# Induced attention, then a gated channel mix: one step for each token-stage operation, stage B inside one PSUM bank, gate products in the sum's bank, second products four steps behind

## The chip, the cores and the metric

The kernel runs on one core of a Trainium2 chip. Its time is the device time of one execution in microseconds (us); lower is better. The engines are TensorE (PE in the profile, its weight loads PEld), VectorE (DVE), ScalarE (ACT), GpSimd (POOL) and SyncE (SP, which here issues nearly all DMAs).

## The reference, cut to what matters

`x` is [4, 12608, 128] in float32, `inducing` is [32, 128], the hidden layer has 1024 columns.

```python
def mab(q, kv):
    s = scale * (q @ kv.transpose(0, 2, 1))
    s = s - s.max(-1, keepdims=True)
    a = np.exp(s)
    a /= a.sum(-1, keepdims=True) + 1e-09
    return a @ kv
h = mab(I, x)              # 32 inducing points attend to all tokens of a batch
x = mab(x, h)              # every token attends to the 32 rows of h
...
x_prev = x shifted by one token, zero at the start
xk = mu_k * x + (1.0 - mu_k) * x_prev
xr = mu_r * x + (1.0 - mu_r) * x_prev
k = np.maximum(xk @ w_k, 0.0)
v = k * k @ w_v
r = 1.0 / (1.0 + np.exp(-(xr @ w_r)))
return r * v
```

## The kernel before

Each of the four batches is cut into 24 groups of 512 tokens and one of 320. A group takes four **steps** of the main loop, one for each pair of 128-column chunks of the hidden layer, so a batch has 100 steps and the program 400. The second attention is never multiplied out: the mixed weights are multiplied by h beforehand (`W[0]`, `W[1]`), and a group's right-hand side `R` holds the 32 softmax weights of each token, as high and low parts in four blocks of 32 partitions, with one column of the group before ("halo") at its left.

One step of a group:
- `up`: four matmuls of 128x512 from `R` and `W` into `ps_a` (two banks wide, two tiles): L760 for the token, L762 for its predecessor, which reads the halo column.
- `square`: VectorE writes `k_t`, the relu of `ps_a` (L772). ScalarE squares it twice, into `k2` in float32 (L773) and into `kh` (L777). GpSimd writes `kl`, the difference of the two (L779). At the steps in `ON_DVE` and `ON_DVE_LAST` VectorE makes `kh` (L775), and at those in `LOW` and `LOW_LAST` it takes 96 of each 512 columns of `kl`.
- `down`: six matmuls (L790) of the step `LAG` = 3 steps back, into the group's sum `ps_v`, from `kh`, `kh` and `kl`.
- Once a group: `zgate` (two matmuls L749, L750 into a `pb_t` bank, and a sigmoid L752), `gate` (L795), `store` (a 32x32 transpose L806 into `ot`, which holds four groups and goes out by four DMAs, L813), and a copy of the halo column on VectorE (L577).

**Token stages** run behind this loop, each of their operations put at a step by `at(step, f)`; what is put at a step is issued at that step's end, after its `down`. *Stage A* of a block (four groups) of the next batch: four 32x32 transposes (`btr`, L326), each followed by four DMAs `xt<-xs`, scores of the inducing points (L355), a maximum common to all partitions (L360, L365 to L372), exponentials (L384, L385), their transpose (L396), and the products for h (L417). *Stage B* of a block of this batch: scores against h (L596), transpose (L603), maximum and subtraction (L607, L610), exponentials (L614), sums, reciprocal and quotient (L618 to L625), transpose back (L630), high and low parts (L634, L638), and 16 DMAs that spread them into four `R` tiles (L647). `SEG` = 12 steps carry one block of A and one of B; six of these segments are followed by 28 steps with `combine`, which finishes h and the next `W`.

Engines execute their own instructions in program order, and each waits for semaphores of the others. The order is written out by hand (`manual_schedule`). All small PSUM tiles share two `pb_t` banks in turn.

## Time and profile before

| what | value |
|---|---|
| median of three runs | 1240.0 us (1239.23 to 1244.31) |
| span of the profiled execution | 1241.0 us (the page has no other time of that execution) |
| PE, PEld busy | 1146.7 us (92%), 828.0 us (67%) |
| DVE busy | 1112.5 us (90%) |
| ACT busy, POOL busy | 960.2 us (77%), 958.2 us (77%) |
| mean granted TensorE clock | 0.991 |
| chain that ended last | PE 48%, DVE 24%, issue 11%, ACT 8%, DMA 5%, SPq 3% |

Busy time is the union of an engine's instructions. A matmul's span is longer than the distance to the next one, since matmuls overlap; so PE can show as busy without being at its peak, and the distance between starts has to be read from the timeline. "Idle before" is the time an engine stood still ahead of a group of instructions, with what ended it.

### The profile page before, as it was taken

What the parts mean: (1) busy time and instruction counts of PE and PEld (TensorE: products, weight loads), DVE (VectorE), ACT (ScalarE), POOL (GpSimd) and SP (SyncE); (2) the same over time, 40 slices, a digit from 0 to 9 for tenths busy, and PEclk for the clock granted to TensorE, in tenths of its full rate; (3) what the DMA queues carried; (4) which work ended last, traced back from release to release, by engine and by line L of the source; (5) the groups of instructions that cost most, each with busy time, mean ns of one, the idle gap of its engine ahead of it and who ended that gap; (6) DMA issues with size and microseconds to landing.
All of it is one profiled execution on the core that took longest, in us unless ns stands there. A gap on an engine that the chain in (4) does not pass through costs nothing.

```text
span 1241.0 us, 17499 instructions
## 1 busy us (share of the span) xinstructions
PE 1146.7 (92%) x5746; PEld 828.0 (67%) x5746; DVE 1112.5 (90%) x1389; ACT 960.2 (77%) x1128; POOL 958.2 (77%) x413
## 2 busy tenths in 40 slices
PE   7789998989999999998989999998999988988997
PEld 5467765766767766666767766666767656666675
DVE  4779999898899999989798999989798999899998
ACT  4478887878778887787878887888777777877885
POOL 1168876878877887877878887777888788877985
PEclk9899999999999999999999999999999999999999
DMA  9122543542333535543315454454133121332222
GB/s 276 40 68 69 124 96 98 132 116 44 55 74 89 124 94 100 118 118 85 70 37 108 106 104 91 106 124 88 36 56 62 24 49 30 68 52 51 40 43 31
DMA packets 260122, 102.25 MB, mean 82 GB/s; under 512 B 219424, under 2 KB 234944, under 8 KB 257728
## 3 DMA queue, kind: packets, MB, share of 16 engines
q1 hardware_dynamic: 259696, 101.12, 37.3%
q8 instruction: 46, 0.75, 0.3%
q14 instruction: 44, 0.36, 0.1%
q10 hardware_dynamic: 336, 0.02, 0.0%
HBM read 28.07 MB, written 25.82 MB: 43 GB/s over the span
## 4 chain that ended last, share of the span: by engine, by line
PE 48%; DVE 24%; issue 11%; ACT 8%; DMA 5%; SPq 3%; POOL 1%; DVEq 0%; ACTq 0%; POOLq 0%
PE ps_v L790 23%; DVE k_t L772 11%; PE ps_a L760 9%; PE ps_a L762 8%; ACT k L773 3%; ACT kh L777 3%; DMA out_dram<-ot 3%; SPq L813 2%; DVE ot L806 2%; PE pb_t L355 2%; DVE kl L779 1%; PE pb_t L596 1%; DVE sm L619 1%; PE pb_t L749 1%; DVE al L638 1%
## 5 line engine op out<-in xcount | busy, mean ns | idle before, releaser
L779 POOL TENSOR_TENSOR kl<-k,kh 128x1024 fp32r<-128x1024 f32 (+4 forms) x400 | 949.5, 2394 | 234.8 <-ACT kh L777 114.2
L773 ACT ACTIVATE k<-k_t 128x1024 f32<-128x1024 f32 (+1 forms) x400 | 417.8, 1045 | 235.3 <-DVE k_t L772 177.1
L772 DVE TENSOR_SCALAR k_t<-ps_a 128x1024 f32<-128x1024 f32 (+1 forms) x400 | 475.2, 1192 | 48.4 <-PE ps_a L762 38.9
L777 ACT ACTIVATE kh<-k_t 128x1024 fp32r<-128x1024 f32 (+1 forms) x379 | 390.4, 1030 | 0.0
L760 PE MATMUL ps_a<-R,W 128*128 128x512 f32 (+1 forms) x800 | 333.9, 418 | 30.5 <-DVE k_t L772 28.8
L762 PE MATMUL ps_a<-R,W 128*128 128x512 f32 (+1 forms) x800 | 316.3, 396 | 14.7 <-DVE R L577 14.7
L790 PE MATMUL ps_v<-kl,wvh 128*128 128x512 f32 (+1 forms) x800 | 252.5, 397 | 7.9 <-POOL kl L779 6.6
L790 PE MATMUL ps_v<-kh,wvh 128*128 128x512 f32 (+1 forms) x800 | 249.2, 393 | 0.0
L790 PE MATMUL ps_v<-kh,wvl 128*128 128x512 f32 (+1 forms) x800 | 248.1, 392 | 0.0
L760 PEld LDWEIGHTS ps_a<-R,W 128*128 128x128 f32 x800 | 151.3, 189 | 127.2 <-DVE k_t L772 64.9
L790 PEld LDWEIGHTS ps_v<-kl,wvh 128*128 128x128 f32 x800 | 143.7, 189 | 57.4 <-POOL kl L779 29.8
L762 PEld LDWEIGHTS ps_a<-R,W 128*128 128x128 f32 x800 | 151.5, 189 | 44.9 <-DVE R L577 19.4
L790 PEld LDWEIGHTS ps_v<-kh,wvh 128*128 128x128 f32 x800 | 150.9, 190 | 34.8
L790 PEld LDWEIGHTS ps_v<-kh,wvl 128*128 128x128 f32 x800 | 150.5, 189 | 34.2
L326 DVE STREAM_TRANSPOSE xs<-xb 128x512 f32<-128x512 f32 x72 | 77.2, 1073 | 8.1 <-DMA xb<-in_x_dram 5.6
L806 DVE STREAM_TRANSPOSE ot<-oT 128x512 f32<-128x512 f32 x96 | 66.6, 694 | 6.5 <-DMA out_dram<-ot 6.4
L795 DVE TENSOR_TENSOR oT<-ps_v,rT 128x512 f32<-128x512 f32 (+1 forms) x100 | 66.9, 669 | 0.7 <-PE ps_v L790 0.7
L752 ACT ACTIVATE rT<-pb_t 128x512 f32<-128x512 f32 (+1 forms) x100 | 57.8, 578 | 0.3
L779 DVE TENSOR_TENSOR kl<-k,kh 128x192 fp32r<-128x192 f32 (+1 forms) x52 | 54.3, 1045 | 3.8 <-ACT kh L777 2.5
L775 DVE TENSOR_TENSOR kh<-k_t 128x1024 fp32r<-128x1024 f32 x21 | 52.8, 2516 | 2.8
L610 DVE TENSOR_TENSOR s<-s,mx 128x512 f32<-128x512 f32 (+1 forms) x27 | 52.8, 1955 | 0.9
L749 PE MATMUL pb_t<-R,W 128*128 128x512 f32 (+1 forms) x100 | 40.8, 408 | 7.0 <-DVE mk L402 3.4
(193 smaller groups left out, 804.0 us busy)
## 6 DMA issues: line engine op xcount, KB each, us to landing
out_dram<-ot SPq DMA_DIRECT2D x92, 256.0 KB, 5.2
xb<-in_x_dram SPq DMA_DIRECT2D x18, 1024.0 KB, 5.2
xt<-xs SPq DMA_DIRECT2D x288, 64.0 KB, 2.0
R<-ah SPq DMA_DIRECT2D x184, 64.0 KB, 2.0
R<-al SPq DMA_DIRECT2D x184, 64.0 KB, 2.0
xb<-in_x_dram SPq DMA_DIRECT2D x8, 256.0 KB, 5.8
kh<-in_x_dram SPq DMA_DIRECT2D x3, 512.0 KB, 7.6
kl<-in_x_dram SPq DMA_DIRECT2D x3, 512.0 KB, 8.0
```

What stands on the lines that cost most here:

```text
L326: nc.vector.transpose(out=xs.rearrange("p (q s) -> p s q", q=M), in_=S.xb[j][:, :, M * c:M * (c + 1)])
L749: nc.tensor.matmul(out=ps[:, :w], lhsT=S.W[0][:, F:WF], rhs=R[:, 1:w + 1], start=True, stop=False)
L752: nc.scalar.activation(out=self.rT, in_=ps[:, :w], func=AF.Sigmoid)
L760: nc.tensor.matmul(out=ps[:, c, :w], lhsT=S.W[0][:, cs], rhs=R[:, 1:w + 1], start=True, stop=False)
L762: nc.tensor.matmul(out=ps[:, c, :w], lhsT=S.W[1][:, cs], rhs=R[:, 0:w], start=False, stop=True)
L772: nc.vector.tensor_scalar(out=k, in0=self.ps[:, :, :w], scalar1=0.0, scalar2=None, op0=ALU.max)
L773: nc.scalar.activation(out=k2, in_=k, func=AF.Square)
L777: nc.scalar.activation(out=kh, in_=k, func=AF.Square)
L779: return lambda eng, a, z: eng.tensor_tensor(out=kl[:, :, a:z], in0=k2[:, :, a:z], in1=kh.bitcast(F32)[:, :, a:z], op=ALU.subtract)
L790: nc.tensor.matmul(out=self.v, lhsT=wt[:, fc, :], rhs=kk[:, c, :], start=(fc == 0 and n == 0), stop=(fc == FC - 1 and n == 2))
L795: nc.vector.tensor_tensor(out=self.oT, in0=self.v, in1=self.rT, op=ALU.mult)
L806: nc.vector.transpose(out=ot[:, o:o + w], in_=self.oT)
```

## The change

**Token stages.** Every operation gets a step of its own, mostly one or two steps after the one that it waits for. Stage A's scores move from step 7 to 9 of a segment, its exponentials from 8 to 16, its last products to 19; stage B's spread of a group's tile moves from steps 16 to 19 to steps 10 to 13, one group a step. In the first batch everything is four steps later. The two PSUM banks become the fixed tiles `pb_a` (stage A, weights) and `pb_b` (stage B, common maximum). Stage B keeps its maximum, its reciprocal and its transposed quotient in its own PSUM bank, where SBUF tiles were. The sums of a row stand two elements apart (`sm3`). Stage A writes its 32x32 blocks contiguously; in return `back` of stage B writes with a stride. The running maximum of stage A moves into a 129th column (`mkr`) of the matrix that is reduced anyway, and the running sum is a `tensor_scalar` with two per-partition operands.

**Main loop.** `LAG` is 4. `k_t`, `kh`, `kl` have four buffers each; `k2` is gone, ScalarE squares `k_t` in place after `kh`. VectorE makes no `kh`, and parts of `kl` at the last three steps alone. `zgate` comes at a group's third step and writes into the `ps_v` bank in which the group's sum starts two steps later. The halo column is copied by a DMA, issued ahead of the group's spread (VectorE copies three of the first batch). `R` has 10 buffers, not 11. ScalarE's order has 61 loads of a function table, where 55 were.

```diff
+    LAG = 4
-    r_pool = ctx.enter_context(tc.tile_pool(name="r_pool", bufs=11))
+    r_pool = ctx.enter_context(tc.tile_pool(name="r_pool", bufs=10))
-    pb = ctx.enter_context(tc.tile_pool(name="pb", bufs=2, space=bass.MemoryType.PSUM))
-    def pb_tile():
-        return pb.tile([P, G], F32, name="pb_t")
+    pb = ctx.enter_context(tc.tile_pool(name="pb", bufs=1, space=bass.MemoryType.PSUM))
+    banks = iter("ab" * 64)
+    def pb_tile(bank=None):
+        return pb.tile([P, G], F32, name="pb_" + (bank or next(banks)))
...
# stage_a
-            nc.vector.transpose(out=xs.rearrange("p (q s) -> p s q", q=M),
+            nc.vector.transpose(out=xs.rearrange("p (s q) -> p s q", q=M),
...
-            if j > 0:
-                nc.vector.tensor_tensor(out=mx, in0=mx, in1=L["mxt"] if tail else S.mrun, op=ALU.max)
...
+        def running():
+            mk = S.mk if j > 0 else sm.tile([P, P + 1], F32, name="mkr", bufs=2)
+            nc.vector.tensor_tensor(out=mk[:, :P], in0=L["cp"][:, :P], in1=apart, op=ALU.add)
+            S.mk = sm.tile([P, P + 1], F32, name="mkr", bufs=2)
+            L["mx"] = S.mk[:, P:P + 1]
+            nc.vector.tensor_reduce(out=L["mx"], in_=mk[:, :P + (j > 0)], op=ALU.max, axis=AX.X)
...
-                nc.vector.scalar_tensor_tensor(out=S.sum, in0=S.sum, scalar=L["al"], in1=L["ss"],
-                                               op0=ALU.mult, op1=ALU.add)
+                nc.vector.tensor_scalar(out=S.sum, in0=S.sum, scalar1=L["al"], scalar2=L["ss"],
+                                        op0=ALU.mult, op1=ALU.add)
...
-            at(t + c + late - 1, lambda c=c: btr(c))
+            at(t + (-1, 0, 1, 3)[c], lambda c=c: btr(c))
-        at(d + 6, scores)
-        at(d + 7, common)
-        at(d + 7, expo)
-        at(d + 9, etrans)
+        at(t + 9, scores)
+        at(t + 10 + tail, common)
+        at(t + 11 + tail, running)
+        at(t + 16, expo)
+        at(t + 17, etrans)
...
# combine
-        at(t + 2, weights)
-        at(t + 3, hfin)
+        at(t + 9, weights)
+        at(t + 10, hfin)
...
-    def halo(S, g):
+    def halo(S, g, far=True):
         if g == 0:
             nc.vector.memset(S.R[g].bitcast(F32)[:, 0:1], 0.0)
+        elif far:
+            nc.sync.dma_start(out=S.R[g].bitcast(F32)[:, 0:1], in_=S.R[g - 1].bitcast(F32)[:, G:G + 1])
         else:
             nc.vector.tensor_copy(out=S.R[g][:, 0:1], in_=S.R[g - 1].bitcast(F32)[:, G:G + 1])
...
# stage_b
-            L["mx"] = sm.tile([P, Q * Q], F32, name="mx2")[:, :nk]
-            nc.vector.tensor_reduce(out=L["mx"], in_=L["s2"], op=ALU.max, axis=AX.X)
+            nc.vector.tensor_reduce(out=L["ps"][:, :nk], in_=L["s2"], op=ALU.max, axis=AX.X)
...
-            L["sm"] = sm.tile([P, Q * Q], F32, name="sm2")[:, :nk]
+            L["sm"] = sm.tile([P, Q * Q, 2], F32, name="sm3", bufs=1)[:, :nk, 0]
...
-            nc.vector.reciprocal(out=L["sm"], in_=L["sm"])
+            nc.vector.reciprocal(out=L["ps"][:, :nk], in_=L["sm"])
...
-            L["aT"] = st.tile([P, G], F32, name="aT")[:, :w]
-            nc.vector.transpose(out=L["aT"], in_=L["s2"].rearrange("p k m -> p (k m)"))
+            L["aT"] = L["ps"][:, :w]
+            if full and b > 0:
+                nc.vector.transpose(out=L["aT"].rearrange("p (q s) -> p s q", q=M), in_=L["s2"])
...
                 S.R[j * Q + i] = r_pool.tile([P, G + 1], F32R, name="R")
+                halo(S, j * Q + i)
...
+        at(t + 1, trans)
+        at(t + 1, maxi)
+        at(t + 2, sub)
+        at(t + 3, expo)
+        at(t + 5, total)
+        at(t + 5, recip)
+        at(t + 6, mult)
+        at(t + 6, back)
+        at(t + 7, high)
+        at(t + 8, low)
         for i in range(Q):
-            at(sp[i], lambda i=i: spread(i))
+            at(t + 9 + i, lambda i=i: spread(i))
...
# Group.zgate, Group.square
-            ps = pb_tile()
+                ps = self.v = pv.tile([P, G], F32, name="ps_v")[:, :w]
...
-            k2 = mp.tile([P, UC, G], F32, name="k2", bufs=2)[:, :, :w]
-            nc.scalar.activation(out=k2, in_=k, func=AF.Square)
-            if dve:
-                nc.vector.tensor_tensor(out=kh, in0=k, in1=k, op=ALU.mult)
-            else:
-                nc.scalar.activation(out=kh, in_=k, func=AF.Square)
+            nc.scalar.activation(out=kh, in_=k, func=AF.Square)
+            nc.scalar.activation(out=k, in_=k, func=AF.Square)
...
# main loop
-                stage_a(b + 1, j, at, s, 3 if b == 0 and j == 0 else 0)
+                stage_a(b + 1, j, at, s)
-            stage_b(b, j + 1, at, s + (5 if b == 0 and j == 0 else 2), s + 7,
-                    [s + 12 + i for i in range(Q)] if last else [s + (16 if j else 12), s + 17, s + 18, s + 19])
+            stage_b(b, j + 1, at, s + 1)
...
-                if n >= NU and u == (1 if grp.g % 3 == 2 else 0):
+                if n >= NU and u == 2:
                     grp.zgate()
```

What that makes of VectorE's order, in the second half of a stage B block (block 0 of the second batch, which runs in the first batch's last 28 steps): `s` is the block's score tile, `sm` its row sums, `kh` and `k_t` the main loop's. Before:

```order
L772 TENSOR_SCALAR k_t<-ps_a 128x1024
L775 TENSOR_TENSOR kh<-k_t 128x1024
L806 STREAM_TRANSPOSE ot<-oT 128x512
L618 TENSOR_REDUCE sm_3517<-s_3353 128x16
L619 TENSOR_SCALAR sm_3517<-sm_3517 128x16
L772 TENSOR_SCALAR k_t<-ps_a 128x1024
L622 RECIPROCAL sm_3517<-sm_3517 128x16
L625 TENSOR_TENSOR s_3353<-s_3353,sm_3517 128x512
L772 TENSOR_SCALAR k_t<-ps_a 128x1024
L577 CAST R<-R 128x1
L630 STREAM_TRANSPOSE aT<-s_3353 128x512
```

VectorE at the same place after:

```order
L785 TENSOR_SCALAR k_t<-ps_a 128x1024
L816 STREAM_TRANSPOSE ot<-oT 128x512
L785 TENSOR_SCALAR k_t<-ps_a 128x1024
L631 TENSOR_REDUCE sm_3497<-s_3404 128x16
L632 TENSOR_SCALAR sm_3497<-sm_3497 128x16
L635 RECIPROCAL pb_b<-sm_3497 128x16
L785 TENSOR_SCALAR k_t<-ps_a 128x1024
L638 TENSOR_TENSOR s_3404<-s_3404,pb_b 128x512
L644 STREAM_TRANSPOSE pb_b<-s_3404 128x16x32
```

The square and the halo copy are gone from between the relus, and reciprocal, quotient and transpose read or write the bank `pb_b`.

SP's order around the DMAs that place x and spread `R`, in a segment of the first batch. Before:

```order
L200 DMA xb<-in_x_dram 128x2048
L194 DMA xl<-in_x_dram 80x4x128
L329 DMA xt<-xs 32x512 x16
L647 DMA R<-ah 32x512
L647 DMA R<-al 32x512
```

SP after, at a block's fourth group:

```order
L664 DMA R<-al 32x512
L336 DMA xt<-xs 32x512 x4
L587 DMA R<-R 128x1
L664 DMA R<-ah 32x512
L664 DMA R<-al 32x512
L664 DMA R<-ah 32x512
L664 DMA R<-al 32x512
L336 DMA xt<-xs 32x512 x8
```

The sixteen `xt<-xs` of a block, which stood together ahead of the sixteen spreads, now stand between them, and ahead of each group's four spreads stands a halo DMA that reads the group before, so it waits for that group's spreads to have landed.

## The prediction

> **What bounds the kernel now.** First the page's busy times, then the windows of the start and of the four batches (columns: window, its us, then busy us of PE, PEld, DVE, ACT and POOL with instruction counts, granted TensorE clock, DMA share, GB/s), then three short stretches in the same view.

> ```profile
> PE 1146.7 (92%) x5746; PEld 828.0 (67%) x5746; DVE 1112.5 (90%) x1389; ACT 960.2 (77%) x1128; POOL 958.2 (77%) x413
> ```

> ```profile
> 0.00:59.00 59.00, 42.32 (x434) 28.25 (x435) 36.73 (x104) 28.90 (x68) 8.71 (x13) 0.97 0.61 166
> 59.00:361.00 302.00, 282.03 (x1414) 202.58 (x1413) 272.23 (x343) 239.58 (x279) 234.42 (x98) 0.98 0.38 86
> 361.00:653.00 292.00, 279.06 (x1399) 201.58 (x1398) 267.93 (x334) 236.22 (x271) 239.16 (x102) 1.00 0.42 93
> 653.00:945.00 292.00, 278.86 (x1396) 201.10 (x1396) 265.99 (x334) 236.20 (x271) 238.64 (x100) 1.00 0.41 89
> 945.00:1241.00 296.00, 264.43 (x1111) 194.51 (x1109) 269.57 (x277) 219.35 (x239) 237.24 (x103) 0.99 0.26 45
> ```

> ```profile
> 395.70:429.30 33.60, 33.31 (x169) 24.12 (x160) 31.82 (x43) 28.05 (x34) 27.03 (x13) 1.00 0.57 126
> 981.50:1018.20 36.70, 32.34 (x136) 23.00 (x135) 34.00 (x34) 27.10 (x31) 30.38 (x12) 1.00 0.32 58
> 575.10:610.50 35.40, 35.40 (x167) 26.05 (x168) 26.55 (x37) 27.34 (x32) 30.36 (x14) 1.00 0.18 41
> 1162.30:1190.60 28.30, 27.57 (x119) 21.63 (x117) 24.52 (x35) 25.77 (x30) 24.97 (x13) 1.00 0.03 7
> ```

> Each short stretch is 12 steps. The last batch, which has no stage A, takes longer (296) than the middle ones, and its usual 12 steps (the second row) 36.7 us; the 12 in which VectorE has neither `kh` to make nor stage B beside it (the last) take 28.3. In the first and third rows TensorE is busy throughout. How much work that is, the distance of starts tells:

> ```profile
> 607.60 0.40 PE L760 MATMUL ps_a<-R,W 128*128 128x512 f32 x1
> ...
> 608.99 0.63 PE L790 MATMUL ps_v<-kh,wvh 128*128 128x512 f32 x2
> 609.46 0.62 PE L790 MATMUL ps_v<-kh,wvl 128*128 128x512 f32 x2
> 609.93 0.62 PE L790 MATMUL ps_v<-kl,wvh 128*128 128x512 f32 x2
> 610.38 0.40 PE L760 MATMUL ps_a<-R,W 128*128 128x512 f32 x1
> ```

> From one L760 to the next step's first stand 12 matmuls (four of `up`, two of the gate, six of `down`) in 2.78 us: 0.232 each. A step is 2.32 us of TensorE, a gate 0.464 in four steps. So a middle batch holds 96 x 2.32 + 24 x 0.464 + 6.1 (42 matmuls of 320 columns, scaled) = 240 us of main work, and spends 292. VectorE's 268 us come in lumps: it is the engine that others wait for, TensorE the one that cannot shrink.

> [...]

> **What leaves VectorE.** By shape:

> ```profile
> L775 DVE TENSOR_TENSOR kh<-k_t 128x1024 fp32r<-128x1024 f32 x21 | 52.8, 2516 | 2.8
> L779 DVE TENSOR_TENSOR kl<-k,kh 128x192 fp32r<-128x192 f32 x49 | 52.3, 1066 | 3.3 <-ACT kh L777 2.0 <-POOL kl L779 0.6 <-issue 0.4
> L610 DVE TENSOR_TENSOR s<-s,mx 128x512 f32<-128x512 f32 x23 | 44.6, 1941 | 0.8
> L625 DVE TENSOR_TENSOR s<-s,sm 128x512 f32<-128x512 f32 x23 | 32.0, 1392 | 0.8
> L638 DVE TENSOR_TENSOR al<-aT,ah 128x512 fp32r<-128x512 f32 x23 | 31.1, 1353 | 1.1 <-ACT ah L634 0.8
> L549 DVE TENSOR_TENSOR al<-pb_t,ah 128x512 fp32r<-128x512 f32 x3 | 2.0, 681 | 0.0
> L619 DVE TENSOR_SCALAR sm<-sm 128x16 f32<-128x16 f32 x23 | 32.7, 1424 | 0.8
> L406 DVE SCALAR_TENSOR_TENSOR sum<-sum,alpha,ss 128x1 f32<-128x1 f32 x15 | 20.2, 1344 | 0.0
> L360 DVE TENSOR_TENSOR mx<-mx,mx 128x1 f32<-128x1 f32 x15 | 16.4, 1094 | 0.5
> L372 DVE TENSOR_SCALAR nb<-mx 128x1 f32<-128x1 f32 x18 | 2.8, 154 | 0.6
> L326 DVE STREAM_TRANSPOSE xs<-xb 128x512 f32<-128x512 f32 x72 | 77.2, 1073 | 8.1 <-DMA xb<-in_x_dram 5.6 <-issue 2.5
> L806 DVE STREAM_TRANSPOSE ot<-oT 128x512 f32<-128x512 f32 x96 | 66.6, 694 | 6.5 <-DMA out_dram<-ot 6.4
> L577 DVE CAST R<-R 128x1 fp32r<-128x1 f32 x96 | 13.2, 138 | 0.0
> L779 POOL TENSOR_TENSOR kl<-k,kh 128x1024 fp32r<-128x1024 f32 x339 | 834.7, 2484 | 198.9 <-ACT kh L777 98.5 <-PE ps_v L790 74.4 <-issue 9.8
> ```

> L610, L625 and L638 read two SBUF tiles and take up to three times as long as L549, the same operation on the same shape with one operand in PSUM; L360 needs 1.1 us for one column. After the change all of these read PSUM or vanish. Gains: 52.8 (`kh`) + 52.3 (`kl`; the last three steps keep theirs) + 23 x (1.941 + 1.392 + 1.353 - 3 x 0.681) = 61 + 23 x (1.424 - 0.154) = 29 + 15 x (1.344 - 0.154) = 18 + 16.4 + 72 x (1.073 - 0.694) = 27 + 13.2 = 270; `back` pays 17 x 0.38 = 6.5 for its stride. VectorE falls from 1112 to about 850; less 37 at the start, 203 a batch. ScalarE gains 21 squares and 6 table loads of about 1.0 and 1.3 us (22 + 8), GpSimd about 45 x 0.4 = 18 at most: 245 and 245 a batch. So TensorE, near 270 us with its small products (the sum below), is alone ahead. `LAG` 4 with four buffers gives every step one step more between `up` and its `kl` product; it removes waits such as these, and costs one more step of products at the end, 6 x 0.145 = 0.9 us:

> ```profile
> POOL kl L779 <- PE ps_v L790: 92.4, 68, 3.9
> PEld ps_v L790 <- POOL kl L779: 29.8, 79, 1.2
> PEld ps_a L762 <- DVE R L577: 19.4, 17, 2.1
> ```

> The third, TensorE waiting for the halo copy, goes too, since the DMA writes the column many steps ahead. Squaring in place and the gate in the sum's bank cost nothing: GpSimd waits for the second square as before, and a bank taken at step 4g+2 and free after 4g+8 is wanted again at 4g+10.

> **What the moved DMAs cost.** SP issues in order:

> ```profile
> 418.71 6.89 SPq L813 DMA_DIRECT2D out_dram<-ot  x4
> 429.55 11.15 SPq L329 DMA_DIRECT2D xt<-xs  x16
> 441.11 0.51 SPq L647 DMA_DIRECT2D R<-ah  x1
> 441.67 0.58 SPq L647 DMA_DIRECT2D R<-al  x1
> ```

> ```profile
> R<-ah SPq DMA_DIRECT2D x184, 64.0 KB, 2.0
> R<-al SPq DMA_DIRECT2D x8, 4.0 KB, 1.7
> xb<-in_x_dram SPq DMA_DIRECT2D x18, 1024.0 KB, 5.2
> ```

> A segment needs 32 issues at 0.63 = 20.2, three quarters of an output = 5.2, one load 0.6, and now four halos 2.5: 28.5 us of its 33.6. A halo waits until the last group's spread has landed, 2.0 - 0.6 = 1.4 us behind its issue, three times a block: 32.7 if no `xt` stands between, less where it does. That fits, barely, and the sixteen `xt` now end about 25 us after the first spread (20 x 0.63 + 16 x 0.63 + 1.4 = 24), seven steps into the segment; the scores at step 9 still find them. Where an output falls among them (one segment in three) its 6.9 us make the scores some 1 to 2 us late, and VectorE's next `store`, which needs `ot` free, 4 to 5 us; TensorE has two `ps_a` tiles of cover and loses perhaps half. I take 4.5 us a batch with stage A, bounds 0 (the cover holds) and 10.

> **The sum**, in the profiled execution (span 1241.0, 1 us over the median 1240.0). Start 59, unchanged. Middle batch: six segments at the TensorE-filled 33.6 = 201.6; 28 steps = 24 x 2.32 + 6 x 0.464 + 6.1 = 64.6, and the weights' products 5.7 (the 35.4 of the third stretch less 12 x 2.32 + 4 x 0.464); 272. First batch the same and the 10 us that it now has over the middle one: 282. Last batch: 240 + 7 score products of about 1 us + 4 for waits = 251, and 10.4 to the end (9.5 now, and the longer drain). 59 + 282 + 2 x 272 + 251 + 10.4 = 1146; plus 3 x 4.5 for SP; less about 10, the halo waits inside the 33.6. **1150 us.**

> **Rivals.**
> 1. *TensorE runs without any wait* (chance 0.2): a segment at 32.4 (1.2 less), no SP loss, last batch 247: 1150 - 18 x 1.2 - 13.5 - 4 = 1111. For it: 28.3 us for 12 steps is reached already. Against: five engines within a fifth of each other.
> 2. *ScalarE's burst* (0.12): exponentials of A and B and a pair of table loads fall in the same step, near 5 us; if a batch's six bursts each hold TensorE for 3 us, 1150 + 18 x 3 = 1204. Against: a step more of cover, and ScalarE's 245 of 272.
> 3. *SP becomes the bound; not faster* (0.06). The place is the halo DMA. Each us by which the three waits of a block pass 1.7 costs 3 us a segment. The gain of 90 is eaten when 18 segments lose 5 each, at waits of 3.5 us; at 4.5 the time is 1150 + 18 x 8.1 = 1296. For it: 5.2 us to landing for large loads; against: 2.0 for spreads, and four `xt` issues (2.5 us) between most. [...]
> 4. *The PSUM operands free nothing* (0.05): then 61 + 29 + 18 of the 270 us stay on VectorE, 230 a batch, still under TensorE but lumpier: if every stage B block costs TensorE one such wait of 1 us, 1150 + 27 = 1177.

> The forecast itself has 0.55 (range 1128 to 1180), an unknown mishap 0.02. From 1110 to 1200 about 0.8 is held. Half a per cent, 6 us, is what a measurement of this kernel can tell from no change: faster 0.92, same 0.02, slower 0.06.

> **What would show it.** PE busy near the whole of every batch and the distance of starts unchanged; DVE near 850; the L610 kind at 0.7 us, the row-sum `tensor_scalar` at 0.2; few waits of TensorE for VectorE or for `xt`; the last batch near 250. I am wrong if SP shows long waits at the halo, if scores wait for `xt`, or if TensorE waits for ScalarE's chain after each burst.

## The result, and the profile after

The changed kernel takes 1226.84 us (median of four runs, 1224.26 to 1232.81), the kernel before 1239.62 on the same chip: ratio 0.990, 95% interval 0.987 to 0.993. It is faster by 12.8 us where 90 were forecast, and outside the forecast range. The profiled execution spans 1224.5 us.

The page's busy times, and the four batches, each from its first relu to the next batch's (columns as in the windows above: window, its us, busy us of PE, PEld, DVE, ACT and POOL, granted clock, DMA share, GB/s):

```profile
PE 1132.5 (92%) x5746; PEld 848.7 (69%) x5746; DVE 875.1 (71%) x1211; ACT 1030.6 (84%) x1155; POOL 949.0 (78%) x413
```

```profile
57.52:362.71 305.19, 279.86 (x1410) 207.16 (x1409) 223.67 (x308) 257.00 (x286) 234.24 (x100) 0.97 0.37 83
362.71:655.71 293.00, 276.49 (x1394) 205.49 (x1394) 216.76 (x295) 252.24 (x276) 235.25 (x100) 0.98 0.43 94
655.71:948.55 292.84, 275.44 (x1397) 204.68 (x1396) 216.94 (x295) 252.25 (x277) 235.52 (x101) 0.99 0.42 89
948.55:1224.50 275.95, 259.75 (x1118) 203.84 (x1116) 180.94 (x211) 240.22 (x250) 235.29 (x101) 0.97 0.28 49
```

The same cuts of the kernel before:

```profile
59.16:361.40 302.24, 282.27 (x1415) 202.77 (x1415) 272.63 (x344) 239.59 (x280) 234.82 (x99) 0.98 0.38 86
361.40:653.03 291.63, 278.69 (x1397) 201.26 (x1397) 267.56 (x334) 236.22 (x272) 238.79 (x101) 1.00 0.42 93
653.03:944.75 291.72, 278.58 (x1395) 200.87 (x1394) 265.71 (x334) 236.19 (x271) 238.36 (x100) 1.00 0.41 89
944.75:1241.00 296.25, 264.68 (x1112) 194.72 (x1110) 269.82 (x277) 219.35 (x239) 237.49 (x103) 0.99 0.26 45
```

VectorE gave up 237 us, and the three batches with a stage A still became 1 to 3 us longer each; the last alone won 20. In those three TensorE is busy for a smaller share than before. What TensorE waited for most before, in the view of waits (who waits, for whom: us in total, times, longest us):

```profile
PE ps_a L760 <- DVE k_t L772: 28.8, 40, 3.3
PE ps_a L762 <- DVE R L577: 14.7, 11, 1.8
```

These are the relu and the halo copy. The waits after, where neither of the two holds a matmul any more:

```profile
PE ps_v L800 <- ACT rT L765: 31.3, 24, 2.2
DVE e L405 <- ACT e1t L394: 25.3, 15, 2.2
PE pb_a L426 <- DVE e L405: 11.6, 8, 3.3
PE pb_b L409 <- ACT s L398: 7.6, 3, 2.5
PE pb_a L341 <- ACT e1t L394: 6.6, 3, 2.2
DVE ot L816 <- DMA out_dram<-ot: 12.9, 4, 4.8
SPq L587 <- DMA R<-al: 40.1, 44, 2.1
```

The first is the gate: the group's second products (L800) may start in their bank only when the sigmoid (L765) has read the gate out of it. The next four hang on stage A's exponentials (L394, L398), which come late: their transpose (L405), the products for h (L426) and, at a batch's last block, two transposes on TensorE (L409, L341). In both cases ScalarE comes last. ScalarE's own timeline at one of the 24 waits (start, us, engine and line), and TensorE's first product behind it:

```profile
1063.92 1.28 ACT L627 ACT_TABLE_LOAD   x1
1065.22 0.63 ACT L627 ACTIVATE s<-s 128x512 f32<-128x512 f32 x1
1065.76 1.04 ACT L786 ACTIVATE kh<-k_t 128x1024 fp32r<-128x1024 f32 x1
1066.83 1.06 ACT L787 ACTIVATE k_t<-k_t 128x1024 f32<-128x1024 f32 x1
1067.80 1.04 ACT L786 ACTIVATE kh<-k_t 128x1024 fp32r<-128x1024 f32 x1
1068.88 1.06 ACT L787 ACTIVATE k_t<-k_t 128x1024 f32<-128x1024 f32 x1
1069.96 1.28 ACT L765 ACT_TABLE_LOAD   x1
1071.25 0.60 ACT L765 ACTIVATE rT<-ps_v 128x512 f32<-128x512 f32 x1
...
1071.90 0.73 PE L800 MATMUL ps_v<-kh,wvh 128*128 128x512 f32 x2 [1.77 <-ACT rT L765]
```

The gate's matmuls ended at 1065.5. ScalarE, which had just spent 1.9 us on a table and an exponential, did four squares first, then loaded the table for the sigmoid: 5.8 us from the gate to its sigmoid, where TensorE wants the bank about 4.5 us after the gate. That is the pattern of these waits. Over the whole trace 24 of the 100 gates have exponentials and a table load between them and their sigmoid, and four squares; it starts 5.4 to 9.3 us after them. The other 76 sigmoids start at most 5.1 us after, most of them 3.0.

And the wait has a tail. The same place in windows, the granted clock third from the right:

```profile
1069.96:1071.90 1.94, 0.17 (x1) 0.00 (x1) 1.94 (x3) 1.93 (x3) 1.94 (x2) 1.00 0.01 4
1071.90:1073.22 1.32, 1.32 (x6) 1.09 (x7) 0.30 (x1) 1.29 (x2) 0.86 (x1) 1.00 0.00 0
1073.22:1076.63 3.41, 3.41 (x10) 2.63 (x9) 1.06 (x1) 3.14 (x4) 2.61 (x2) 0.50 0.00 0
1076.63:1084.00 7.37, 7.37 (x33) 5.98 (x32) 4.18 (x6) 6.09 (x7) 6.46 (x3) 1.00 0.23 52
```

After the wait TensorE has 3.41 us at half its clock: another 1.7 us. Over the span the clock costs up to (1 - 0.977) x 1224.5 = 28 us, and up to 11 before:

```profile
core 0: 1241.0 us, clock 0.991
```

```profile
core 0: 1224.5 us, clock 0.977
```

### The profile page after: what moved, and what is told of

Read it like the earlier page. It is cut to its first block, busy times and chain, and to the rows that moved or that the text cites. A ratio compares the mean times of both kernels' runs of the same rounds, so it can differ in the third digit from the quotient of the medians.

```text
span 1224.5 us, 17466 instructions
## 1 busy us (share of the span) xinstructions
PE 1132.5 (92%) x5746; PEld 848.7 (69%) x5746; DVE 875.1 (71%) x1211; ACT 1030.6 (84%) x1155; POOL 949.0 (78%) x413
## 4 chain that ended last, share of the span: by engine, by line
PE 66%; ACT 16%; DVE 7%; issue 5%; DMA 3%; SPq 2%; POOL 0%; DVEq 0%; ACTq 0%; POOLq 0%
PE ps_v L800 34%; PE ps_a L773 12%; PE ps_a L775 11%; ACT kh L786 5%; ACT k_t L787 3%; DVE k_t L785 3%; ACT L765 2%; PE pb_b L610 2%; PE ps_v L762 1%; PE ps_v L763 1%; PE pb_a L361 1%; ACT L393 1%; ACT rT L765 1%; ACT e1t L394 1%; DMA out_dram<-ot 1%
## 5 line engine op out<-in xcount | busy, mean ns | idle before, releaser
L789 POOL TENSOR_TENSOR kl<-k_t,kh 128x1024 fp32r<-128x1024 f32 (+2 forms) x400 | 940.3, 2367 | 228.0 <-ACT k_t L787 168.8
L786 ACT ACTIVATE kh<-k_t 128x1024 fp32r<-128x1024 f32 (+1 forms) x400 | 417.6, 1044 | 137.0 <-PE ps_v L800 86.5
L787 ACT ACTIVATE k_t<-k_t 128x1024 f32<-128x1024 f32 (+1 forms) x400 | 419.3, 1048 | 12.7
L775 PE MATMUL ps_a<-R,W 128*128 128x512 f32 (+1 forms) x800 | 319.5, 400 | 0.0
L800 PE MATMUL ps_v<-kh,wvh 128*128 128x512 f32 (+1 forms) x800 | 256.0, 402 | 31.3 <-ACT rT L765 31.3
L800 PE MATMUL ps_v<-kh,wvl 128*128 128x512 f32 (+1 forms) x800 | 252.2, 397 | 0.0
L800 PE MATMUL ps_v<-kl,wvh 128*128 128x512 f32 (+1 forms) x800 | 250.7, 395 | 0.0
L773 PEld LDWEIGHTS ps_a<-R,W 128*128 128x128 f32 x800 | 154.0, 193 | 75.7 <-issue 21.4
L800 PEld LDWEIGHTS ps_v<-kh,wvh 128*128 128x128 f32 x800 | 151.6, 193 | 76.2 <-ACT rT L765 42.6
L800 PEld LDWEIGHTS ps_v<-kh,wvl 128*128 128x128 f32 x800 | 153.1, 192 | 35.6
L775 PEld LDWEIGHTS ps_a<-R,W 128*128 128x128 f32 x800 | 154.7, 193 | 30.7
L800 PEld LDWEIGHTS ps_v<-kl,wvh 128*128 128x128 f32 x800 | 151.3, 190 | 35.1
L765 ACT ACTIVATE rT<-ps_v 128x512 f32<-128x512 f32 (+1 forms) x99 | 57.2, 578 | 0.3
L333 DVE STREAM_TRANSPOSE xs<-xb 128x512 f32<-128x512 f32 x72 | 50.0, 694 | 3.1 <-DMA xt<-xs 2.6
L762 PE MATMUL ps_v<-R,W 128*128 128x512 f32 (+1 forms) x99 | 39.4, 398 | 0.0
L763 PE MATMUL ps_v<-R,W 128*128 128x512 f32 (+1 forms) x99 | 39.3, 397 | 0.0
L426 PE MATMUL pb_a<-xb,e 128*32 128x128 f32 x576 | 23.3, 279 | 11.7 <-DVE e L405 11.6
## 6 DMA issues: line engine op xcount, KB each, us to landing
xb<-in_x_dram SPq DMA_DIRECT2D x18, 1024.0 KB, 5.1
```

What stands on the lines that cost most here:

```text
L762: nc.tensor.matmul(out=ps[:, :w], lhsT=S.W[0][:, F:WF], rhs=R[:, 1:w + 1], start=True, stop=False)
L763: nc.tensor.matmul(out=ps[:, :w], lhsT=S.W[1][:, F:WF], rhs=R[:, 0:w], start=False, stop=True)
L765: nc.scalar.activation(out=self.rT, in_=ps[:, :w], func=AF.Sigmoid)
L773: nc.tensor.matmul(out=ps[:, c, :w], lhsT=S.W[0][:, cs], rhs=R[:, 1:w + 1], start=True, stop=False)
L775: nc.tensor.matmul(out=ps[:, c, :w], lhsT=S.W[1][:, cs], rhs=R[:, 0:w], start=False, stop=True)
L786: nc.scalar.activation(out=kh, in_=k, func=AF.Square)
```

## The experiments

Each kernel is the changed one with the edit shown, unless said; ratios are against the kernel before on the same chip. That kernel took 1238.95 to 1241.54 us on the chips used, so a difference in us between two kernels from different chips can be 2 to 3 us off.

**Gate a step earlier.** Three steps instead of two between the gate and the first product in its bank.

```diff
-                if n >= NU and u == 2:
+                if n >= NU and u == 1:
                     grp.zgate()
```

> The gate's two matmuls and the sigmoid come at a group's second step instead of its third (three steps ahead of the group's first second product, not two); all else is the changed kernel. Theory W (TensorE loses its time to second products that wait for the sigmoid to have read the bank that they overwrite, 48.8 us of late L800 starts in the profile): these waits fall under 10 us and the time to about 1187 us. Rival A (ScalarE's chain is the bound, the wait at the bank is only where it shows): the waits move to the kl products, the relu and the scores, and the time stays within 1210 to 1230 us.

1199.47 us, 0.966 (0.964 to 0.968): 27.4 us off by one digit. The wait for the sigmoid is gone from the longest waits. In its place the gate waits for the bank itself, which the group before gives back late, but for less:

```profile
PE ps_v L762 <- DVE oT L805: 7.4, 11, 1.9
```

**Exponentials of stage A two steps earlier**, with the gate as changed.

```diff
-        at(t + 16, expo)
+        at(t + 14, expo)
```

> Stage A's exponentials come at step 14 of a segment instead of 16, so no longer in the step of stage B's, with as many table loads; all else is the changed kernel. Theory T (the chain exponentials, transpose, products for h, and the last block's TensorE work behind the exponentials in bank a, is one step too tight: L426 15.4, L409 8.0, L341 7.0 us of late starts): these three fall from 30 to under 8 us and the time to about 1203 us. Rival A (ScalarE is the bound): the time stays within 1218 to 1232 us, since ScalarE has the same work.

1205.26 us, 0.969 (0.966 to 0.973): 21.6 us. The waits at L409 and L341 are gone, three at L426 are left (8.6 us), and the one for the sigmoid stands (27.0 us in 22). So these are two separate waits, behind the same engine.

**Both.**

> Both of the former edits together. Theories W and T together: about 1165 us (40 and 23 us less than the changed kernel's 1227). Rival A: 1205 to 1230 us. If the gains overlap (the split burst alone already lets the sigmoid come in time): as fast as the better of the two alone.

1187.86 us, 0.956 (0.953 to 0.960). Of 27.4 + 21.6 = 49.0 us 39.0 arrive. What comes next shows in the waits and on SP, where an output that was stored at 459.8 is issued at 467.6, behind eight `xt`, a halo and four spreads:

```profile
DVE ot L816 <- DMA out_dram<-ot: 23.4, 8, 4.8
```

```profile
459.22 2.49 SPq L336 DMA_DIRECT2D xt<-xs  x4
461.87 0.51 SPq L587 DMA_DIRECT2D R<-R  x1
462.42 0.60 SPq L664 DMA_DIRECT2D R<-ah  x1
...
467.56 4.45 SPq L823 DMA_DIRECT2D out_dram<-ot  x4
```

**No table loads.** The exponentials of the main loop's stages A and B are sigmoids, so ScalarE needs one table; the softmax weights are other numbers.

```diff
-            nc.scalar.activation(out=L["s2"], in_=L["s2"], func=AF.Exp, scale=scale)
+            nc.scalar.activation(out=L["s2"], in_=L["s2"], func=AF.Sigmoid, scale=scale)
...
```

> The exponentials of stages A and B in the main loop are replaced by sigmoids (another function of the same shape, so the numbers are not the reference's): ScalarE loads a function table 2 times instead of 61, 76 us less work for it; all else is the changed kernel. Rival A (ScalarE's amount of work is the bound): the time falls by about the 76 us, to 1150 us. Theory W and T (only the lateness of a few ScalarE results counts): the late starts of L800 fall from 49 to under 15 us, those of L426, L409 and L341 from 30 to about 12, and the time to about 1175 us, not lower than the two schedule edits together by more than 20 us.

1172.4 us, 0.945 (0.942 to 0.947). The trace of the changed kernel holds 62 loads of 1.283 us, this one 2: ScalarE has 77 us less to do, and the kernel is 54 us shorter. TensorE's wait for the sigmoid falls to 4.1 us in 8. The order was left as it is, so the gate's place alone does not make the bank late; it takes the table loads in front of the sigmoid too.

**Halo columns by VectorE again** (on top of both), except at a block's first group: SP loses three issues and three waits a block.

```diff
-                halo(S, j * Q + i)
+                if i == 0:
+                    halo(S, j * Q)
...
-                    if nxt.b == 0 and nxt.g < Q:
+                    if nxt.g % Q or (nxt.b, nxt.g) == (0, 0):
                         halo(nxt.S, nxt.g, far=False)
```

> The kernel of both schedule edits (1188 us), with the halo columns of three groups in four copied by VectorE again, two steps ahead of the group, so that 69 of the 93 halo DMAs and their waits leave SP's queue. Theory S (SP's queue is the next limit: outputs queue behind spreads and halos, VectorE waits for the output tile, 23 us, and TensorE loses 5 us a time): SP runs about 10 us less behind, those waits fall to under 12 us and the time to 1176 us. Rival H (the halo copy on VectorE costs TensorE again what it cost before, some 19 us of waits ahead of L775): 1190 to 1205 us.

1171.36 us, 0.946 (0.942 to 0.949): 16.5 us less than with both alone.

**Two output tiles of two groups** (on top of both), so that a store need not wait for the output before it.

```diff
-        return mp.tile([P, Q * G], F32, name="ot", bufs=1)
+        return mp.tile([P, 2 * G], F32, name="ot", bufs=2)
```

> The kernel of both schedule edits (1188 us), with two output tiles of two groups each instead of one of four, and so an output's four DMAs for every second group, half as large and twice as many. Theory S: VectorE's waits for the output tile (23 us, 8 times) are gone, the long segments (38 to 39 us where 33.6 is usual, one a batch) too: about 1170 us. Rival Q (the doubled issues crowd SP's queue and the x blocks come late): 1185 to 1200 us, with waits of the scores for xt.

1165.52 us, 0.941 (0.939 to 0.944): 22.3 us less than with both, and below both kernels by 5 to 6%. Its middle segments are full, at the length that the forecast used:

```profile
385.00:418.70 33.70, 33.70 (x180) 24.53 (x176) 27.95 (x38) 30.45 (x34) 29.46 (x14) 1.00 0.57 127
418.70:452.40 33.70, 33.70 (x184) 24.50 (x176) 28.17 (x39) 30.79 (x35) 28.68 (x13) 1.00 0.46 110
```

**All four edits.**

> Gate at the second step, exponentials two steps earlier, halo columns within a block by VectorE, two output tiles of two groups. The earlier two edits on top of the first pair were worth 16.5 us (halo) and 22.3 us (output) apart. Theory S (both removed the same collision of SP's halo and output issues with the spreads): the gains overlap almost wholly, 1160 to 1166. Theory Q (two independent delays): they add, 1187.9 - 16.5 - 22.3 = 1149.

1167.17 us, 0.942 (0.938 to 0.947), no better than without the halo edit: the two remove one collision, as theory S has it.

**LAG 3**, with the gate at the second step, so again two steps ahead of the products.

```diff
-    LAG = 4
+    LAG = 3
...
-                if n >= NU and u == 2:
+                if n >= NU and u == 1:
```

> The changed kernel with LAG 3 (second products three steps behind, as before the change; four buffers stay), and the gate a step earlier, so that gate and first second product stand two steps apart as in the changed kernel. Theory W (the two steps between gate and first second product are what costs): L800 waits for the sigmoid as in the changed kernel, near 45 us, and the time 1220 to 1240 us. Rival L (the fourth step carried the gain of the change): kl products wait for GpSimd, over 30 us, and the time is 1245 us or more.

1254.96 us, 1.014 (1.011 to 1.017). The total is theory L's, the reason is not: TensorE waits for the sigmoid (54.6 us in 27, L765), not for `kl`. The products that come a step sooner meet a bank that ScalarE is just as late to read.

**Stage B's maximum, sums, reciprocal and quotient in SBUF tiles again.**

```diff
-            nc.vector.tensor_reduce(out=L["ps"][:, :nk], in_=L["s2"], op=ALU.max, axis=AX.X)
+            L["mx"] = sm.tile([P, Q * Q], F32, name="mx2")[:, :nk]
+            nc.vector.tensor_reduce(out=L["mx"], in_=L["s2"], op=ALU.max, axis=AX.X)
...
-            L["aT"] = L["ps"][:, :w]
+            L["aT"] = st.tile([P, G], F32, name="aT")[:, :w]
```

> The changed kernel with stage B's maximum, row sums, reciprocal and transposed quotient in SBUF tiles again, as before the change. VectorE gets back some 90 us, 875 to about 965. Theory W (TensorE does not wait for VectorE here, so the operands' place bought little): 1225 to 1240 us. Rival V (VectorE's lumps delay the relu, and with it all): 1250 us or more.

1274.4 us, 1.030 (1.026 to 1.033). So the bank's operands are worth 47.6 us, and the theory that room on VectorE bought little falls. Two small things go with the edit: the row sums stand side by side again, and the tile `aT` also serves an output, so that VectorE waits 7.6 us for its DMA. Subtraction, quotient and low part, here and then in the changed kernel (mean ns of one is the number behind the busy us):

```profile
L624 DVE TENSOR_TENSOR s<-s,mx 128x512 f32<-128x512 f32 x23 | 46.3, 2012 | 0.0
L639 DVE TENSOR_TENSOR s<-s,sm 128x512 f32<-128x512 f32 x23 | 50.5, 2195 | 0.0
L655 DVE TENSOR_TENSOR al<-aT,ah 128x512 fp32r<-128x512 f32 x23 | 38.8, 1687 | 0.0
```

```profile
L623 DVE TENSOR_TENSOR s<-s,pb_b 128x512 f32<-128x512 f32 x23 | 15.1, 658 | 0.0
L638 DVE TENSOR_TENSOR s<-s,pb_b 128x512 f32<-128x512 f32 x23 | 15.5, 675 | 0.0
L654 DVE TENSOR_TENSOR al<-pb_b,ah 128x512 fp32r<-128x512 f32 x23 | 15.4, 671 | 0.0
```

VectorE's 978 us are still not the bound. TensorE waits for L766, the sigmoid there, for 49.5 us where it was 31.3. That the lumps of 2 us delay the relu, with it the squares and so the sigmoid behind them is how I read it; the waits show only its end. What the 2 us go with stands in the last section.

**One part alone, on the kernel before: VectorE makes no `kh` and no part of `kl`.**

```diff
-    ON_DVE = (68, 86, 88)
-    ON_DVE_LAST = (8, 10, 20, 22, 32, 34, 44, 46, 56, 58, 68, 70)
+    ON_DVE = ()
+    ON_DVE_LAST = ()
...
-    LOW = range(91, 97)
-    LOW_LAST = [*range(60, 66), *range(72, 97)]
+    LOW = ()
+    LOW_LAST = ()
```

> The kernel before with one part of the change alone: VectorE makes no kh and takes no columns of kl; ScalarE squares twice at every step and GpSimd writes all of kl. VectorE gives up 53 + 52 us, ScalarE gains 30, GpSimd 18. Theory V (the last batch's 36.7 us for 12 steps is VectorE's 24 us of squares and the lumps behind them): the last batch falls by 10 to 20 us and the total to 1218 to 1230. Rival G (the squares stood on VectorE because GpSimd's 2.5 us a step and ScalarE's chain have no room with three steps of cover): 1240 to 1265, with TensorE waiting for kl or kh at the down products.

1201.01 us, 0.970 (0.965 to 0.974): more than theory V gave, and 26 us faster than the whole change. 24 steps of its last batch, ahead of them the same steps of the kernel before:

```profile
981.53:1054.83 73.30, 64.54 (x270) 45.87 (x269) 67.89 (x65) 54.09 (x60) 60.74 (x24) 1.00 0.22 44
```

```profile
963.40:1028.95 65.55, 63.03 (x270) 46.76 (x268) 52.99 (x61) 57.61 (x63) 59.87 (x24) 1.00 0.25 49
```

It wins 30 us in the last batch (266.2 from its first relu to the end) and 2 to 6 in each of the others.

**The wait filled.** In the last batch, ahead of the six late products, TensorE gets seven matmuls that nobody reads.

```diff
+            if n - (B - 1) * UB in range(8, 69, 12):
+                ps = pb_tile("a")
+                for _ in range(7):
+                    nc.tensor.matmul(out=ps, lhsT=grp.S.W[0][:, :P], rhs=grp.S.R[grp.g][:, 1:G + 1], start=True, stop=True)
             if old is not None:
                 old.down(ou)
```

> The changed kernel with 42 more matmuls: in the last batch, at each of the six places where TensorE waits about 2 us for the bank behind the sigmoid, seven 128x512 matmuls into the idle pb_a fill 7 x 0.233 = 1.63 us of that wait; nobody reads them. In the profile of the changed kernel five of those waits are followed within 1.4 us by 3.41 us at a granted clock of 0.50, which costs 1.7 us each. Theory C (the wait costs twice, once as idleness and once by the clock that it lowers): the five low stretches vanish, 12 steps take 32.4 us instead of 34.1, the kernel is 8 to 9 us faster than 1226.8, near 1218, with more work in it. Rival N (the clock falls for another reason): the low stretches stay, 1226 to 1230.

1220.85 us, 0.986 (0.982 to 0.989): 6 us less, with 42 more matmuls. 12 steps of the last batch, in the changed kernel and then here:

```profile
1015.28:1049.43 34.15, 32.38 (x136) 24.82 (x135) 23.06 (x27) 30.25 (x32) 28.64 (x13) 0.95 0.20 43
```

```profile
1014.34:1046.97 32.63, 32.51 (x143) 25.01 (x142) 23.06 (x27) 30.05 (x32) 28.64 (x13) 1.00 0.24 46
```

The low clock is gone from these segments, and 1.5 us each with it. From its first relu to the end the last batch takes 268.3 us where it took 276.0; what stands ahead of it is 2 us longer, hence 6 and not 8. The intervals of the two kernels' ratios overlap (0.982 to 0.989, 0.987 to 0.993), so the proof lies in these rows more than in the totals.

**The same seven matmuls four steps later** (`range(12, 73, 12)`), where TensorE does not wait.

> The control: the same 42 matmuls four steps later, at the next group's first second product, where the changed kernel's TensorE does not wait. Theory C: the waits and the low stretches behind them stay and the work comes on top, 6 x 1.63 = 9.8 us: near 1236, or less where the delay gives ScalarE time and shortens the next waits. If this too comes out at 1218, it was the shift in time that helped and not the filling.

1233.18 us, 0.995 (0.992 to 0.997): 6.3 us slower than the changed kernel, 12.3 slower than the filled wait with intervals clear of each other, so it was not the shift in time that helped. As a control it is not clean. The waits stayed, but four of the five low stretches went, since the segments, now 34.3 us, fall differently on the clock's raster (last section): these four waits leave 1.4 to 1.9 us of idleness in any one window of the raster, where the five of the changed kernel leave 2.0 to 2.1. The 1.6 us of matmuls took the place of the 1.7.

## Why the prediction missed

**The step that failed** is "Squaring in place and the gate in the sum's bank cost nothing: ... a bank taken at step 4g+2 and free after 4g+8 is wanted again at 4g+10." It asked when the bank is free for the next group. It did not ask when this group's own sum may start: at 4g+4, and only once the sigmoid of 4g+2 has run, which at 24 gates stands in ScalarE's order behind four squares, exponentials and a table load. Before, the gate went into a `pb_t` bank, and no matmul of that kernel waited for its sigmoid (L752), only three weight loads did, for 1.0 us in all. So the bank did cost something: 31.3 us of waits, and one step of distance is worth 27.4 us.

**Rival 2 had the mechanism.** ScalarE's lumps are what TensorE waits for, in 24 waits at the gate and 14 behind stage A's exponentials. It gave 3 us each to 18 bursts, 54 us in all, and 1204, but named no place where TensorE would wait. The price was near: the two edits of the order return 39 us, the table loads 54. I argued it away with "ScalarE's 245 of 272", a mean. ScalarE is at 252 of 293 in the middle batches, and a 5.8 us chain inside them still came 2 us late.

**Each wait was priced once.** No term had the clock in it. Of the 57.8 us between the profiled changed kernel and the one with all four edits (1166.7), (1 - 0.977) x 1224.5 less (1 - 0.992) x 1166.7 = 19 are clock at most, by this row and that of the changed kernel:

```profile
core 0: 1166.7 us, clock 0.992
```

**SP's term was a little small, inside its bounds.** 4.5 us a batch, 13.5 in all (bounds 0 and 30), for outputs among the spreads; removing that collision gave 16.5, 22.3 and, with both remedies, 20.7 us. These runs are from other chips than the kernel that they are compared with; by the ratios it is 13, 19 and 17. The place was right, also the way (an output issued 8 us after its store, the next store waiting up to 4.8). The halo DMAs of 4 B a partition land 1.7 us after their issue (64 KB spreads 2.0), and the waits for what they read are at most 2.1 us, below the 3.5 of rival 3. (That rival's 8.1 us a segment at waits of 4.5 is a slip: its own 3 x (4.5 - 1.7) is 8.4, and the time 1301.)

**LAG** was to remove waits for `kl`. It is worth 28 us against LAG 3 with the same two steps to the gate's bank, for the most part through that bank (31.3 us of waits against 54.6).

**What held.** The spacing of matmuls is 0.233 us. VectorE is at 875 where 850 were forecast. The L610 kind takes 0.66 to 0.68 us, so rival 4, by which PSUM operands free nothing, is out; no matmul waits for relu or halo copy any more. A segment of the kernel with two output tiles is 33.7 (33.6 forecast), and the last batch with all four edits runs 260.2 us from its first relu to the end (251 + 10.4 forecast). "If TensorE waits for ScalarE's chain after each burst" was named as what would make me wrong, and did. In time: 1150 forecast, 1167 with all four edits, 1227 without. Of the last 17 us, 9 lie in the first batch (290.9 against 282), 5 and 7 in the middle ones (277.3 and 278.9 against 272), less 1 in the last and the 3.5 that the forecast added (13.5 - 10); no run took them apart.

**Where VectorE's gain went.** Taking the squares and the parts of `kl` off it gives 39 us alone. The change as a whole gives 13, because what TensorE had waited for on VectorE it now waits for on ScalarE: from the first relu on, what matmuls start later than 0.24 us behind the one before, half clock included, sums to 149 us before and 139 after, and to 78 with all four edits.

## What to carry to other kernels

When a small result is put into the bank of a larger sum, count the distance from its matmul to the sum's first product, and in between everything that its reader's engine does first, table loads too; an engine's mean load says nothing of that. Look for the next wait on the engine that the work was moved to. Where TensorE waits about 2 us at a stretch, add up to 1.7 us for the clock (3.41 us at a granted 0.50 followed five of six such waits in the last batch here), and let a DMA queue that carries several streams have a second buffer for the one that comes in lumps.

## What was not expected of the hardware

The subtraction, quotient and low part with both operands in SBUF took 1.9, 1.4 and 1.4 us in the kernel before and 2.0, 2.2 and 1.7 in the experiment with the same tiles; with one operand in PSUM they took 0.66 to 0.68. The traces show what the length goes with: GpSimd's difference `kl` beside them. First a low part of the experiment, then a quotient of the changed kernel, each started while `kl` was being written:

```profile
405.54 2.40 POOL L790 TENSOR_TENSOR kl<-k_t,kh 128x1024 fp32r<-128x1024 f32 x1 [5.59 <-ACT k_t L788]
405.99 2.51 DVE L655 TENSOR_TENSOR al<-aT,ah 128x512 fp32r<-128x512 f32 x1
```

```profile
1068.03 2.40 POOL L789 TENSOR_TENSOR kl<-k_t,kh 128x1024 fp32r<-128x1024 f32 x1 [1.54 <-ACT k_t L787]
1069.06 0.68 DVE L638 TENSOR_TENSOR s<-s,pb_b 128x512 f32<-128x512 f32 x1
```

The first ends 0.56 us after GpSimd's instruction, the second before it. Of the 126 full-width ones with two SBUF operands that started beside a running `kl`, 123 ended 0.5 to 0.6 us after it; the nine that met none took 0.67 to 0.69 us. All 66 of the changed kernel that started beside one took 0.65 to 0.68.
